# Two rows of maxima issued from ScalarE's queue, and two more banks in a ring of score banks

## The chip, the cores and the metric

The kernel runs on one core of a Trainium2 chip. The metric is the device time of one execution in microseconds. Engines are named as the profile names them: PE (TensorE, matmuls; PEld its weight loads), DVE (VectorE), ACT (ScalarE), POOL (GpSimd) and SP (SyncE, which here only issues DMAs). A queue is the list of instructions of one engine, taken in order.

## What is computed

Four layers on x of 2048 x 576: attention A, spectral layer B, and both again with the same weights. Only A is touched.

```python
def _A_ref(x, wqkv, wo):                      # on the layernorm of x
    B, S, D = x.shape
    H = 32; Dh = D // H; W = 256
    q, k, v = ...(x @ wqkv)...                 # 32 heads of 18
    scores = einsum("bhqd,bhkd->bhqk", q, k) * (Dh ** -0.5)
    mask = (idx[:, None] - idx[None, :] >= 0) & (idx[:, None] - idx[None, :] < W)
    p = softmax(where(mask, scores, -1e9))
    return einsum("bhqk,bhkd->bhqd", p, v)... @ wo
x = x + _A_ref(_layernorm(x), A_wqkv, A_wo)
x = x + _B_ref(_layernorm(x), ...)             # FFT, product, inverse FFT
```

## The kernel before

`layer_a` is called twice. Its first part normalises x, transposes it and makes v. Its second part, in which the change lies, is one loop over steps t (line 908), from -10 to 129. The 32 heads form 8 groups n of 4; a group has 16 tiles of 128 positions, and step t stands for tile j = t mod 16 of group n = t // 16.

In a step t from 0 to 127, `exps` makes for each of four heads the scores of key tile j against the query tiles j to j+2 by one matmul into a PSUM bank (E, L843), ACT's exponential of it into the tile `P` (L844), and POOL masks `P` (L846, L849). `pv` (L863) multiplies the `P` of two steps earlier with v into the bank `U`. In the same step `score_max` runs ten tiles ahead, for tile x = t + 10: a matmul of raw scores into a bank (S, L811) and a masked maximum over keys by DVE (L813) into a column of `m`. So the ten steps before step 0, called the lead here, hold maxima alone. After every fourth tile, `m_rows` transposes a chunk of 16 columns of `m` (four heads, four tiles; `tpm`, L819), ACT negates them into `mt` (L821), and four DMAs of 2 KB, one per head, put them as an extra row into the query tile `qs` (L826), where the matmul of E adds them to the scores, the keys holding ones in that row. E of step j needs the rows of query tile j+2: steps 0 and 1 need chunk 0, steps 2 to 5 chunk 1, steps 6 to 9 chunk 2. Chunks 0 and 1 of group 0 are finished in the lead, in steps -6 and -2. Every fourth step also has `norm`, which divides the results of a chunk (`tpo`, L873, L876, L878) and stores them to `o_d` (L883).

The projections to q and k (`proj`, L750) run in pieces between the steps up to step 102; `goal` says how many pieces stand after which step. Each ends in two banks `pj`, which ACT copies (L758), DVE adds (L762) and POOL splits into high and low part (`sg`, L763, L764); the result is stored to `qk_d` in DRAM (512 KB, L765) and comes back, sorted by head, as twelve loads of 72 KB per group and chunk (`stack_load`, L790, six for `qs`, six for `ks`). For the pieces made in the lead, `sg` lies in the five buffers of `P`: the exponentials of steps 0 to 4 each overwrite one of them and so wait until its store has landed. `sg2_0` is the projection piece i = 2, c = 0, and so on; `mt0_1` is group 0, chunk 1.

PSUM has 8 banks: three with the tag S, two E, two pj, one U. `bank` gives S, E, `tpm` and `tpo` their banks; in the lead S alone, from step 0 a ring of five: S, S, E, E, S.

Instructions stand on each engine in the order in which the code is written; nothing moves them but the code. Where a DMA is issued from, SP's queue or ACT's, is written in the code as well. The program that is built gives each such DMA one of eight completion counters, DMAHW0 to DMAHW7, in turn, one count for both queues, in an order of the whole program that the build chooses; a DMA waits until the DMA before it on its counter has landed.

At the end, `room` (step 104) loads the output projection's weights `wo` (L474, 2.9 MB a layer), and in steps 125 to 127 `turn` takes pj banks for transposes of the output (`tpa`, L499, L500, read by DVE in L504, L505).

Of the kernel before, what the change touches and what calls it, by code (L numbers as in the profile page):

```python
# [8 lines left out]
F32 = mybir.dt.float32  # L9
# [6 lines left out]
S, D = 2048, 576  # L16
# [559 lines left out]
def layer_a(tc, src, dst, wqk_d, wv_d, wo_d, dc_d, gc_d, dram, copy, wvs, wos, second, spectral):  # L576
    nc = tc.nc
# [8 lines left out]
    with ExitStack() as ctx:  # L586
# [129 lines left out]
        with ExitStack() as c2:  # L716
            wp = c2.enter_context(tc.tile_pool(name="a2", bufs=2))
            pp = c2.enter_context(tc.tile_pool(name="a2p", bufs=2, space=PSUM))
# [7 lines left out]
            for j in range(2):  # L726
                q = wp.tile([128, 2, S], F32R, name=f"qs{j}", bufs=1)
# [41 lines left out]
                            rest()  # L769
                return [lambda s=s, k=k: mm(s, k) for s, k in enumerate(ks)]  # L770

            turns, later = [0], []

            def bank(name):

                turns[0] += t >= 0
                return pp.tile([128, 512], F32, name=name, **(dict(tag="E", bufs=2) if turns[0] % 5 > 2 else dict(tag="S", bufs=3)))

            vts = {}

            def stack_load(n, c):

                q, k = qs[n % 2], ks_[n % 2]
                cs = slice(c * 512, c * 512 + 512)
                for which, t, parts in ((0, q, (0, 0, 1)), (1, k, (0, 1, 0))):
                    for hp in range(2):
                        r0 = 144 * n + 72 * which + 36 * hp
                        for slot, part in enumerate(parts):
                            b = 64 * hp + 18 * slot
                            nc.sync.dma_start(t[b:b + 18, :, cs].bitcast(F32),  # L790
                                              qk_d[part, r0:r0 + 36, cs].rearrange("(f d) t -> d f t", f=2).bitcast(F32))

            def v_load(n):
                v = wp.tile([128, NT, 4, 19], F32, tag="vq", name=f"vq{n}", bufs=2)
                nc.sync.dma_start(v.rearrange("p b h e -> p (b h e)"), v_d[n].rearrange("p b e -> p (b e)"))
                vts[n] = v
# [3 lines left out]
            def score_max(x, pair, hp):  # L800

                n, i = divmod(x, NT)
                c, t = divmod(i, 4)
                q, k = qs[n % 2], ks_[n % 2]
                if t == hp == pair == 0:
                    ms[n, c] = wp.tile([128, 2, 2, 4], F32, tag="m", name=f"m{n}_{c}", bufs=3)
                lo, hi = max(0, i - 2) * 128, (i + 1) * 128
                N = hi - lo
                b = 64 * hp
                ps = bank(f"S{x}_{pair}_{hp}")  # L810
                T.matmul(ps[:, 0:N], q[b:b + 63, pair, i * 128:i * 128 + 128], k[b:b + 63, pair, lo:hi], start=True, stop=True)  # L811
                jk = wp.tile([128, 384], BF, tag="jk", name=f"jk{x}_{pair}_{hp}", bufs=3)
                V.tensor_tensor_reduce(out=jk[:, 0:N], in0=ps[:, 0:N], in1=mask[:, 384 - N:384], scale=1.0, scalar=-3e38,  # L813
                                       op0=ALU.add, op1=ALU.max, accum_out=ms[n, c][:, hp, pair, t:t + 1])

            def m_rows(n, c):
                q = qs[n % 2]
                tp = bank(f"tpm{n}_{c}").rearrange("p (a t) -> p a t", a=4)
                T.transpose(tp[0:16, 0], ms[n, c].rearrange("p a b t -> p (a b t)"), ident)  # L819
                mt = wp.tile([16, 128], F32R, tag="mt", name=f"mt{n}_{c}", bufs=2)  # L820
                A.activation(mt, tp[0:16, 0], AF.Copy, scale=-1.0)  # L821
                for hp in range(2):
                    for pair in range(2):
                        r = (hp * 2 + pair) * 4
                        b = 64 * hp + 63
                        nc.sync.dma_start(q[b:b + 1, pair, c * 512:c * 512 + 512].rearrange("a (t q) -> a t q", t=4).bitcast(F32),  # L826
                                          mt[r:r + 4].bitcast(F32))

            pt = {}

            def exps(x, pair, hp):

                n, j = divmod(x, NT)
                q, k = qs[n % 2], ks_[n % 2]
                nq = min(3, NT - j) * 128
                hl_ = 2 * hp + pair
                if hp == pair == 0:
                    pt[n, j] = wp.tile([128, 4, 384], F32, tag="P", name=f"P{n}_{j}", bufs=5)
                p = pt[n, j]

                ps = bank(f"E{x}_{hl_}")
                b = 64 * hp
                T.matmul(ps[:, 0:nq], k[b:b + 64, pair, j * 128:j * 128 + 128], q[b:b + 64, pair, j * 128:j * 128 + nq], start=True, stop=True)  # L843
                A.activation(p[:, hl_, 0:nq], ps[:, 0:nq], AF.Exp, scale=SC)  # L844
                if hp == pair == 1:
                    P.affine_select(out=p[:, :, 0:128], in_=p[:, :, 0:128], pattern=[[0, 4], [1, 128]], compare_op=ALU.is_ge,  # L846
                                    fill=0.0, base=0, channel_multiplier=-1)
                    if nq == 384:
                        P.affine_select(out=p[:, :, 256:384], in_=p[:, :, 256:384], pattern=[[0, 4], [-1, 128]], compare_op=ALU.is_gt,  # L849
                                        fill=0.0, base=0, channel_multiplier=1)  # L850
# [45 lines left out]
            pj = [f for i in range(2, 9) for c in range(4) for f in proj(i, c, "E" if i == 2 and c % 2 else "pj", True)]  # L896
            done = 0

            goal = {t: -(-70 * (t + LEAD + 1) // 9) if t < -1 else (75, 80, 84)[t + 1] for t in range(-LEAD, 2)}
            for m in range(22):  # L900
                a, b = [2 + 23 * z // 5 for z in (m, m + 1)]
# [6 lines left out]
            for t in range(-LEAD, NX + 2):  # L908

                if t + LEAD in (0, 2):  # L910
                    stack_load(0, 2 + (t + LEAD) // 2)
                n, c = divmod(t + 20, NT)
                if c % 4 == 0 and 0 < n < NQ:
                    stack_load(n, c // 4)
                if t + LEAD == 5:
                    v_load(0)
                if t + 12 in range(NT, NX, NT):
                    v_load((t + 12) // NT)

                want = goal.get(t, len(pj))  # L920
                more, done = pj[done:want], want
                for pair in range(2):
                    for hp in range(2):
                        if 0 <= t < NX:
                            exps(t, pair, hp)
                    for hp in range(2):
                        if t + LEAD < NX:
                            score_max(t + LEAD, pair, hp)
                    while later:
                        later.pop()()  # L930
                    if pair == 0 and 0 <= t - 2 < NX:
                        pv(t - 2)
                    if pair == 0 and t < 2:
                        for f in more[:(len(more) + 1) // 2]:
                            f()
                        more = more[(len(more) + 1) // 2:]
                for f in more:
                    f()
                if copy and t >= 32 and t % 4 == 0 and t < 32 + 16 * len(copy):

                    z, r = divmod(t // 4 - 8, 4)
                    P.dma_start(*[a[32 * r:32 * r + 32] for a in copy[z]])

                y = t + LEAD - 1
                if 0 <= y < NX and y % 4 == 3:
                    m_rows(*divmod(y // 4, 4))
                y = t - 3
                if 0 <= y < NX - 1 and y % 4 == 3:
                    norm(*divmod(y // 4, 4))
                if t == OB - 16:  # L950
                    out.room()
                if t - OB in (0, 1, 2):
                    out.load(t - OB)
                if t == OB + 3:
                    out.consts()
                    out.last(slice(96, 128), slice(0, 56))
                if t == NX - 1:
                    out.last(slice(0, 96), slice(0, 128))

                if t - OB - 4 in (0, 1, 2, 4):  # L960
                    out.tail(min(t - OB - 4, 3))
                if t - OB - 5 in (0, 1, 2):
                    u = t - OB - 5
                    out.turn(u, pp.tile([128, 512], F32, tag="pj", name=f"tpa{u}", bufs=2), V)
                    if u < 2:
                        out.load(u + 3)
                if t == NX:

                    A.activation(wp.tile([128, 1], F32, name="se", bufs=1), eps, AF.Sqrt)
# [61 lines left out]
```

## Time and profile before

| | us |
|---|---|
| runs | 1547.83, 1542.71, 1542.78; median 1542.78 |
| the profiled execution | 1542.73 |
| its span, first to last instruction | 1540.7 |
| PE busy in the span | 1403.2 (91%) |
| DVE, ACT, POOL busy | 962.1, 815.6, 726.1 |
| matmuls E / S (L843 / L811), 1024 each | 233.2 / 234.2 |
| DVE masked maxima (L813), 1024 | 500.0 |
| ACT exponentials (L844), 1024 | 423.2 |

In the first attention layer, E of step 0 starts 132.32 us after the span's start, step 103 at 429.62, step 112 at 453.13 and step 118 at 468.15; in the second layer the same steps start at 901.38, 1198.03, 1221.55 and 1236.60.

How to read it: a row of a timeline gives start, length, engine, line, operation, out<-in, shape and count, and in brackets the idle time of the engine ahead of it with what ended it. A row of a windows table gives the stretch, its length, busy time and number of instructions of PE, PEld, DVE, ACT and POOL, then PE's granted clock as a share of full speed, the busy share of the DMA engines, and GB/s. A row of waits gives who waited for whom, the total, how many times, and the longest. Rows with a q behind the engine's name (SPq) are issues of DMAs: their length is the time of issue, not of the transfer.

### The profile page before, as it was taken

To read this page: it belongs to the slowest core of one execution; us is meant where nothing else is said; L and a number is where in the kernel's file an instruction comes from. 1 tells how busy PE (TensorE), PEld (TensorE's weight loads), DVE (VectorE), ACT (ScalarE), POOL (GpSimd) and SP (SyncE) were. 2 spreads that over 40 slices of the span, in tenths; PEclk is the share of its full clock that TensorE was granted. 3 is DMA by queue.
4 is the path that set the end of the run, shared out by engine and by line. 5 is a ranking of instruction groups with operands and counts; after the bars stand their busy time and mean duration, and the time that the engine had idled before them with its cause. 6 is when DMAs were issued, how large, how long until landed. Compare 5 with 4: busy or idle time off the path is not lost. (4 is left out here: it accounts for less than half of the span.)

```text
span 1540.7 us, 35484 instructions
## 1 busy us (share of the span) xinstructions
PE 1403.2 (91%) x12312; PEld 1071.6 (70%) x12312; DVE 962.1 (62%) x3103; ACT 815.6 (53%) x1895; POOL 726.1 (47%) x1215
## 2 busy tenths in 40 slices
PE   7997999999999899877789979999999998998677
PEld 7985666666656798537689856666666567985376
DVE  5356787788884555445443567878888835554445
ACT  6523767677666444225455236777666654442254
POOL 3364566566544333244611646565555443332445
PEclk9998999999999999988989989999999999999889
DMA  7856456555555366666374565555445553656663
GB/s 235 266 172 213 151 166 183 165 169 160 158 166 151 123 219 199 224 198 203 135 226 114 178 212 152 163 157 155 147 140 156 158 150 119 223 191 224 194 207 135
DMA packets 197423, 271.81 MB, mean 176 GB/s; under 512 B 87294, under 2 KB 109438, under 8 KB 196030
## 3 DMA queue, kind: packets, MB, share of 16 engines
q1 hardware_dynamic: 185502, 250.65, 52.3%
q10 hardware_dynamic: 10976, 15.59, 3.0%
q0 software_dynamic: 768, 3.31, 0.8%
q8 instruction: 99, 1.62, 0.5%
q14 instruction: 78, 0.64, 0.1%
HBM read 167.88 MB, written 103.86 MB: 176 GB/s over the span
## 5 line engine op out<-in xcount | busy, mean ns | idle before, releaser
L813 DVE CUSTOM_DVE_ANT_0 jk<-S,mask 128x384 bf16<-128x384 f32 (+2 forms) x1024 | 500.0, 529 | 111.5 <-PE S L811 106.9
L844 ACT ACTIVATE P<-E 128x384 f32<-128x384 f32 (+2 forms) x1024 | 423.2, 476 | 187.2 <-PE E L843 157.0
L846 POOL TENSOR_SCALAR_AFFINE_SELECT P<-P 128x512 f32<-128x512 f32 x256 | 162.3, 634 | 295.2 <-ACT P L844 277.8
L843 PE MATMUL E<-qs,ks 64*128 64x384 f32 (+2 forms) x1024 | 233.2, 400 | 21.8 <-DMA qs<-mt 15.3
L811 PE MATMUL S<-ks,qs 63*128 63x384 f32 (+2 forms) x1024 | 234.2, 367 | 3.3 <-DMA wqr<-in_wqk 1.9
L863 PE MATMUL U<-P,vq 128*19 128x128 f32 (+1 forms) x3840 | 202.9, 329 | 1.0 <-POOL P L849 1.0
L843 PEld LDWEIGHTS E<-qs,ks 64*128 64x128 f32 x1024 | 123.9, 184 | 106.2 <-issue 44.3
L750 PE MATMUL pj<-xh,wqh 64*128 64x512 f32 (+1 forms) x640 | 165.9, 405 | 2.1 <-ACT vt L710 1.7
L811 PEld LDWEIGHTS S<-ks,qs 63*128 63x128 f32 x1024 | 130.8, 186 | 44.8 <-ACT P L844 20.3
L863 PEld LDWEIGHTS U<-P,vq 128*19 128x19 f32 x3840 | 89.9, 98 | 93.5 <-issue 34.5
L849 POOL TENSOR_SCALAR_AFFINE_SELECT P<-P 128x512 f32<-128x512 f32 x224 | 142.0, 634 | 0.0
L750 PE MATMUL pj<-xl,wqh 64*128 64x512 f32 (+1 forms) x512 | 128.4, 395 | 0.0
L750 PE MATMUL pj<-xh,wql 64*128 64x512 f32 (+1 forms) x640 | 120.6, 392 | 0.0
L522 PE MATMUL ops<-oroom 128*128 128x288 f32 x784 | 113.7, 301 | 4.4 <-DVE oroom L505 3.0
L522 PEld LDWEIGHTS ops<-oroom 128*128 128x128 f32 x784 | 106.6, 191 | 6.2 <-DVE oroom L505 4.0
L171 POOL TENSOR_TENSOR eo<-xn 128x287 f32<-128x287 f32 x32 | 26.1, 817 | 148.2 <-ACT xn L169 148.2
L750 PEld LDWEIGHTS pj<-xh,wqh 64*128 64x128 f32 (+1 forms) x640 | 88.0, 188 | 7.4 <-ACT vt L710 2.1
L813 DVE DVE_READ_ACCUMULATOR2_ANT m<- 128x1 f32 x1024 | 85.0, 83 | 0.0
L199 PE MATMUL pf<-dc,et 128*128 128x290 f32 x384 | 72.4, 313 | 9.6 <-DVE et L190 6.5
L750 PEld LDWEIGHTS pj<-xh,wql 64*128 64x128 f32 (+1 forms) x640 | 72.2, 186 | 7.7
L764 POOL TENSOR_TENSOR sg<-sg 128x512 fp32r<-128x512 f32 x56 | 72.0, 1286 | 4.7
L750 PEld LDWEIGHTS pj<-xl,wqh 64*128 64x128 f32 (+1 forms) x512 | 71.3, 189 | 3.7
(181 smaller groups left out, 2555.4 us busy)
## 6 DMA issues: line engine op xcount, KB each, us to landing
qk_d<-sg SPq DMA_DIRECT2D x56, 512.0 KB
qs<-qk_d SPq DMA_DIRECT2D x384, 72.0 KB
ks<-qk_d SPq DMA_DIRECT2D x384, 72.0 KB
v_d<-vt SPq DMA_DIRECT2D x32, 304.0 KB
vq<-v_d SPq DMA_DIRECT2D x16, 608.0 KB
yd<-ye SPq DMA_DIRECT2D x32, 290.0 KB
wt<-in_w SPq DMA_DIRECT2D x16, 580.0 KB
x<-ofree SPq DMA_DIRECT2D x32, 288.0 KB
```

What stands on the lines that cost most here:

```text
L171: P.tensor_add(eo[:, 0, 1:288], xn[:, 1:288], xn[:, 575:288:-1])
L199: T.matmul(o, et[:, c, si], m(5 * c + mi), start=q == 0, stop=False)
L522: self.nc.tensor.matmul(self.ps[u][n][:, 0:288], x, self.w[p][:, wk * D + n * 288:wk * D + n * 288 + 288], start=first and i == 0, stop=la ...
L750: T.matmul(ps, w[r, wk], xT(xk, cs)[r], start=s == 0, stop=s == len(ks) - 1)
L764: (P if halves else V).tensor_sub(sg[:, 1], su, sg[:, 0].bitcast(F32))
L811: T.matmul(ps[:, 0:N], q[b:b + 63, pair, i * 128:i * 128 + 128], k[b:b + 63, pair, lo:hi], start=True, stop=True)
L813: V.tensor_tensor_reduce(out=jk[:, 0:N], in0=ps[:, 0:N], in1=mask[:, 384 - N:384], scale=1.0, scalar=-3e38, op0=ALU.add, op1=ALU.max, accu ...
L843: T.matmul(ps[:, 0:nq], k[b:b + 64, pair, j * 128:j * 128 + 128], q[b:b + 64, pair, j * 128:j * 128 + nq], start=True, stop=True)
L844: A.activation(p[:, hl_, 0:nq], ps[:, 0:nq], AF.Exp, scale=SC)
L846: P.affine_select(out=p[:, :, 0:128], in_=p[:, :, 0:128], pattern=[[0, 4], [1, 128]], compare_op=ALU.is_ge, fill=0.0, base=0, channel_mult ...
L849: P.affine_select(out=p[:, :, 256:384], in_=p[:, :, 256:384], pattern=[[0, 4], [-1, 128]], compare_op=ALU.is_gt, fill=0.0, base=0, channel ...
L863: T.matmul(U[32 * h:32 * h + 19, (q0 % 4) * 128:(q0 % 4) * 128 + 128 * (q1 - q0)], vts[n][:, j, h], pt[n, j][:, h, (q0 - j) * 128:(q1 - j) ...
```

## The change

Two edits. The rows of chunks that are finished before step 2, which are chunks 0 and 1 of group 0 in each layer, are issued from ACT's queue. And the ring becomes a list that is turned; after the last step with a projection (102), the two pj banks are put at its head, so that it has seven banks from step 103 on.

```diff
-            turns[0] += t >= 0
-            return pp.tile([128, 512], F32, name=name, **(dict(tag="E", bufs=2) if turns[0] % 5 > 2 else dict(tag="S", bufs=3)))
+            banks, later = ["S", "S", "E", "E", "S"], []
+            def bank(name):
+                tag = "S"
+                if t >= 0:
+                    banks.append(tag := banks.pop(0))
+                return pp.tile([128, 512], F32, name=name, tag=tag, bufs=3 if tag == "S" else 2)
...
-                        nc.sync.dma_start(q[b:b + 1, pair, c * 512:c * 512 + 512].rearrange("a (t q) -> a t q", t=4).bitcast(F32),
-                                          mt[r:r + 4].bitcast(F32))
+                        (nc.sync if t >= 2 else nc.scalar).dma_start(q[b:b + 1, pair, c * 512:c * 512 + 512].rearrange("a (t q) -> a t q", t=4).bitcast(F32),
+                                                                     mt[r:r + 4].bitcast(F32))
...
+                if t == max(goal) + 1:
+                    banks[:0] = ["pj", "pj"]
```

No instruction changes its place on PE, DVE or POOL. On ACT, in the first layer, eight DMAs come in (names in brackets are what an instruction waits for; lines are two higher than before):

```order
L823 ACTIVATE mt0_0_1483<-tpm0_0_1481 16x128 [waits PE_49]
L828 DMA qs0_1051<-mt0_0_1483 1x4x128 [waits DMAHW1_49,Activation_49,Pool_49]
L828 DMA qs0_1051<-mt0_0_1483 1x4x128 [waits DMAHW2_49]
L828 DMA qs0_1051<-mt0_0_1483 1x4x128 [waits DMAHW4_49]
L828 DMA qs0_1051<-mt0_0_1483 1x4x128 [waits DMAHW5_49]
L758 COPY sg2_2_1505<-pj2_2_0_1434 128x512 [waits PE_49]
L758 COPY sg2_3_1585<-pj2_3_0_1507 128x512 [waits PE_49]
L758 COPY sg3_0_1646<-pj3_0_0_1587 128x512 [waits PE_49]
L823 ACTIVATE mt0_1_1654<-tpm0_1_1652 16x128 [waits PE_49]
L828 DMA qs0_1051<-mt0_1_1654 1x4x128 [waits DMAHW1_49,Activation_49,Pool_49]
L828 DMA qs0_1051<-mt0_1_1654 1x4x128 [waits DMAHW3_49]
L828 DMA qs0_1051<-mt0_1_1654 1x4x128 [waits DMAHW4_49]
```

A twelfth row of the kind, the fourth DMA of `mt0_1`, waits for DMAHW6, and behind it stands the first exponential of step 0. Before, the same rows of ACT held the two `mt` and the three copies alone. On SP the loads of the last chunk of group 0 and the stores behind them now read:

```order
L792 DMA ks0_1052<-qk_d_70 18x2x512 [waits DMAHW7_49]
L792 DMA ks0_1052<-qk_d_70 18x2x512 [waits DMAHW0_49]
L792 DMA ks0_1052<-qk_d_70 18x2x512 [waits DMAHW1_49]
L792 DMA ks0_1052<-qk_d_70 18x2x512 [waits DMAHW2_49]
L792 DMA ks0_1052<-qk_d_70 18x2x512 [waits DMAHW3_49]
L792 DMA ks0_1052<-qk_d_70 18x2x512 [waits DMAHW4_49]
L765 DMA qk_d_70<-sg2_0_1348 128x2x512 [waits DMAHW5_49,Pool_49]
L765 DMA qk_d_70<-sg2_1_1420 128x2x512 [waits DMAHW6_49,Pool_49]
L604 DMA wqr5_1463<-in_wqk 128x640 [waits DMAHW7_49,Pool_49]
L797 DMA vq0_1489<-v_d_71 128x1216 [waits DMAHW0_49]
L765 DMA qk_d_70<-sg2_2_1505 128x2x512 [waits DMAHW1_49,Pool_49]
```

Before, four rows `qs0<-mt0_0` stood between `wqr5` and `vq0`, and the loads waited for other loads of SP. In the change, the DMAs ahead of the third, fifth and sixth load on their counters (1, 3, 4) are the first three DMAs of `mt0_1` on ACT, and the one ahead of the store of `sg2_1` (6) is the fourth; the counters' values in the built program say so. In the same way the last four loads of the chunk before wait, three of them, for DMAs of `mt0_0`.

On PE, the second place is step 113: the E and S matmuls of heads 0 and 2, those of U with the `P` of steps 110 and 111 between them, and E and S of heads 1 and 3. In the change it reads:

```order
L845 MATMUL E113_0_7791<-qs1_1053,ks1_1054 128x384 [waits Activation_49]
L845 MATMUL E113_2_7794<-qs1_1053,ks1_1054 128x384 [waits DVE_49]
L813 MATMUL S123_0_0_7797<-ks1_1054,qs1_1053 128x384 [waits DVE_49]
L813 MATMUL S123_0_1_7801<-ks1_1054,qs1_1053 128x384 [waits Activation_49]
L865 MATMUL U_1055<-P6_14_7655,vq6_6304 19x256 [waits Pool_49]
L865 MATMUL U_1055<-P6_14_7655,vq6_6304 19x256 x3
L865 MATMUL U_1055<-P6_15_7713,vq6_6304 19x128 [waits Pool_49]
L865 MATMUL U_1055<-P6_15_7713,vq6_6304 19x128 x3
L845 MATMUL E113_1_7815<-qs1_1053,ks1_1054 128x384 [waits Activation_49]
L845 MATMUL E113_3_7818<-qs1_1053,ks1_1054 128x384 [waits DVE_49]
L813 MATMUL S123_1_0_7823<-ks1_1054,qs1_1053 128x384 [waits DVE_49]
L813 MATMUL S123_1_1_7827<-ks1_1054,qs1_1053 128x384 [waits Activation_49]
```

The same matmuls before:

```order
L843 MATMUL E113_0_7791<-qs1_1053,ks1_1054 128x384 [waits DVE_49]
L843 MATMUL E113_2_7794<-qs1_1053,ks1_1054 128x384 [waits Activation_49]
L811 MATMUL S123_0_0_7797<-ks1_1054,qs1_1053 128x384 [waits Activation_49]
L811 MATMUL S123_0_1_7801<-ks1_1054,qs1_1053 128x384 [waits DVE_49]
L863 MATMUL U_1055<-P6_14_7655,vq6_6304 19x256 [waits Pool_49]
L863 MATMUL U_1055<-P6_14_7655,vq6_6304 19x256 x3
L863 MATMUL U_1055<-P6_15_7713,vq6_6304 19x128 [waits Pool_49]
L863 MATMUL U_1055<-P6_15_7713,vq6_6304 19x128 x3
L843 MATMUL E113_1_7815<-qs1_1053,ks1_1054 128x384 [waits DVE_49]
L843 MATMUL E113_3_7818<-qs1_1053,ks1_1054 128x384 [waits Activation_49]
L811 MATMUL S123_1_0_7823<-ks1_1054,qs1_1053 128x384 [waits Activation_49]
L811 MATMUL S123_1_1_7827<-ks1_1054,qs1_1053 128x384 [waits DVE_49]
```

The order is the same, and each matmul now waits for the reader of the bank seven back, an exponential or a maximum of the step before, where it waited for the one five back.

More of the change, by code (lines that the diff above doesn't have):

```diff
@@ L770, in proj @@
                 return [lambda s=s, k=k: mm(s, k) for s, k in enumerate(ks)]
-            turns, later = [0], []
+            banks, later = ["S", "S", "E", "E", "S"], []
             def bank(name):
-                turns[0] += t >= 0
-                return pp.tile([128, 512], F32, name=name, **(dict(tag="E", bufs=2) if turns[0] % 5 > 2 else dict(tag="S", bufs=3)))
+                tag = "S"
+                if t >= 0:
+                    banks.append(tag := banks.pop(0))
+                return pp.tile([128, 512], F32, name=name, tag=tag, bufs=3 if tag == "S" else 2)
             vts = {}
```

## Prediction

> **What bounds the kernel now.** I start from the page, whose first line is the profiled execution's span.
>
> ```profile
> span 1540.7 us, 35484 instructions
> ```
>
> That execution took 1542.73 us, so 2.0 us lie outside its span; it stands 0.05 us under the median of the three runs, 1542.78. The sum below is made against 1542.73. Next I read the list of waits for the tile that the change touches, the rows of maxima `mt`.
>
> ```profile
> PE E L843 <- DMA qs<-mt: 15.3, 2, 7.8
> ```
>
> Two waits, one in each attention layer, 15.3 us together. The timeline of PE shows the first of them, at step 2 of the first layer; the last row is step 6.
>
> ```profile
> 144.87 1.02 PE L843 MATMUL E<-qs,ks 64*128 64x384 f32 x2 [7.85 <-DMA qs<-mt]
> ...
> 145.82 1.02 PE L843 MATMUL E<-qs,ks 64*128 64x384 f32 x2
> ...
> 157.51 0.44 PE L843 MATMUL E<-qs,ks 64*128 64x384 f32 x2
> ```
>
> So PE stands from 137.0 to 144.9. The windows around it (the seventh column is the granted clock) show what the stall costs behind itself.
>
> ```profile
> 137.00:139.00 2.00, 0.02 (x2) 0.00 (x0) 1.32 (x5) 0.58 (x1) 1.79 (x3) 1.00 0.59 166
> 141.00:143.00 2.00, 0.00 (x0) 0.00 (x0) 0.00 (x0) 0.00 (x0) 0.00 (x0) 0.50 1.02 382
> 149.00:151.00 2.00, 2.00 (x22) 0.96 (x21) 0.65 (x3) 1.14 (x3) 0.00 (x0) 0.59 0.78 233
> ```
>
> The clock is half from 141 to about 150.5, so some 5.5 us of work run at half speed and lose about half of that. I put 1.9 us of it on the wait, as the steps after it are not all bound by the clock: 9.7 us a layer hang on these rows.
>
> Why are they late? SP's own timeline, in order of issue, and the two engines that feed it:
>
> ```profile
> 123.08 2.62 SPq L790 DMA_DIRECT2D ks<-qk_d  x6
> 125.80 0.89 SPq L765 DMA_DIRECT2D qk_d<-sg  x2
> ...
> 128.01 2.96 SPq L826 DMA_DIRECT2D qs<-mt  x4
> ...
> 131.99 3.13 SPq L790 DMA_DIRECT2D qs<-qk_d  x6
> 136.03 3.93 SPq L790 DMA_DIRECT2D ks<-qk_d  x6
> 140.06 0.90 SPq L765 DMA_DIRECT2D qk_d<-sg  x2
> 141.05 3.15 SPq L826 DMA_DIRECT2D qs<-mt  x4
> ...
> 149.71 2.50 SPq L826 DMA_DIRECT2D qs<-mt  x4
> ```
> ```profile
> 120.27 0.27 ACT L821 ACTIVATE mt<-tpm 16x128 fp32r<-16x128 f32 x1 [3.56 <-PE tpm L819]
> 121.34 0.59 ACT L758 COPY sg<-pj 128x512 f32<-128x512 f32 x1 [0.81 <-PE pj L750]
> ...
> 130.15 0.26 ACT L821 ACTIVATE mt<-tpm 16x128 fp32r<-16x128 f32 x1
> 132.81 0.87 ACT L844 ACTIVATE P<-E 128x384 f32<-128x384 f32 x2 [2.40 <-issue]
> ```
> ```profile
> 122.72 0.68 DVE L762 TENSOR_TENSOR sg<-sg,pj 128x512 f32<-128x512 f32 x1
> ```
>
> The rows of chunk 1 are ready on ACT at 130.41 and issued at 141.05: 10.6 us in SP's order, behind stores of projections and loads of the next group. That is the wait.
>
> **The lead, part by part.** *Removed from SP:* eight issues a layer, which took 2.96 + 3.15 = 6.1 us of its time. *Added to ACT:* the same eight, undisturbed 2.50 / 4 = 0.62 us each, so 2.5 us behind each `mt`. Chunk 0: ACT is free again at 123.0, and the copy of 121.34 is 1.7 us late; DVE's addition at 122.72 needs it, and starts about 1.0 us late, with the maxima queued behind it. I let between nothing and 0.7 us of this reach `mt` of chunk 1. Chunk 1: ACT issues until 132.9 or 133.6; the exponentials of 132.81 give way by under 1 us. Taken alone the rows of chunk 1 would land near 134.5, ahead of the 137.0 at which PE asks for them.
>
> *What takes the place of the wait.* SP and ACT draw the completion counters of their DMAs from the same eight, and a DMA waits until the one before it on its counter has landed. In the order of the change, the third, fifth and sixth of the six `ks` loads that stood at 123.08 follow the first three `mt` rows of chunk 1 on their counters, and the second store of `sg2` follows the fourth. So those loads, and all behind them on SP, now wait for rows that ACT issues after 130.4. The third row is issued at about 131.7 to 132.4 and ends 0.6 later. To land it takes at most 1.6 us: in the trace it was issued by 143.6 and the second matmul of the pair at 144.87, which needs it, had started before 145.82; I take 1.5. So it lands at 133.8 to 134.5, and the stores of 125.80 go out at about 134.2 to 134.9, over 8 us late.
>
> The rest of SP's chain, from those stores to the first row of chunk 2, took 149.71 - 125.80 = 23.9 us; without the eight issues, 17.8. So chunk 2 is issued from 152.0 to 152.7 instead of 149.71, and is usable 3.8 us later (as 141.05 to 144.87): step 6, which needs it, starts at 155.8 to 156.5 where it now starts at 157.51. PE itself would be there sooner: exponentials of step 0 overwrite the tiles that those stores read. Two stores and a row behind them were through in 4.8 us (140.06 to 144.87), so they hold step 0 until 137 to 139, PE stands about 4 us there once its banks are full, and 3.3 us for the rest of steps 0 and 1 (132.8 to 137.0, less the first pair) and 12.6 us for steps 2 to 5 (144.87 to 157.51) bring it to about 153.5. Chunk 2 is what comes last, and the layer gains 1.0 to 1.7 us of the 9.7; I take 1.2.
>
> Ends: the two groups of six loads at 131.99 and 136.03 took 7.1 us with their waits; if these shrink by 2.5 us, chunk 2 and PE's own path meet at 153.7, a gain of 3.8. If instead the stores and loads, now closer together, delay each other by 3 us more, the layer loses 2. So -3.8 to +2 a layer, nearer the first estimate since it keeps the chain's measured length; **-2.4 for both**.
>
> The Trainium skill, DMA: Bandwidth & Descriptors, section Issuing engines are not separate DMA queues, says that issuing from several engines saves only the sequencer's time of issue. By that rule the move would be worth at most the 6.1 us of SP's time a layer, -12.2 in all; by the rows above ACT's queue does pass 10.6 us of SP's order, and the counters take it back. No run here shows a row on ACT's queue.
>
> **The ring after step 102.** Steps 103 on, by windows (PE, PEld, DVE, ACT, POOL):
>
> ```profile
> 440.00:451.00 11.00, 10.24 (x104) 5.64 (x105) 9.30 (x37) 7.40 (x21) 4.92 (x9) 1.00 0.88 307
> ...
> 453.00:468.00 15.00, 13.91 (x135) 7.69 (x133) 12.98 (x52) 10.59 (x27) 6.74 (x11) 1.00 0.12 23
> 468.00:472.00 4.00, 3.69 (x47) 1.96 (x43) 1.82 (x8) 3.40 (x10) 1.80 (x3) 1.00 0.02 6
> 472.00:484.00 12.00, 10.67 (x141) 5.61 (x129) 0.71 (x2) 11.46 (x30) 8.38 (x16) 1.00 0.63 177
> ```
> ```profile
> 455.46 0.33 PE L843 MATMUL E<-qs,ks 64*128 64x384 f32 x1
> 456.02 0.44 PE L843 MATMUL E<-qs,ks 64*128 64x384 f32 x1 [0.23 <-ACT P L844]
> ```
>
> No engine is full, and the second E of a pair starts 0.56 us after the first: its bank waits for the exponential five banks back. Seven banks remove that. But up to step 112 the gain cannot be kept:
>
> ```profile
> 441.72 1.94 SPq L474 DMA_DIRECT2D oroom<-wos  x4
> 443.90 2.49 SPq L826 DMA_DIRECT2D qs<-mt  x4
> ```
> ```profile
> SPq L826 <- DMA oroom<-wos: 5.3, 4, 1.7
> ```
> ```profile
> 453.13 0.74 PE L843 MATMUL E<-qs,ks 64*128 64x384 f32 x2
> ```
>
> Step 112 (453.13) needs the rows issued at 443.90, which stand behind the loads of `wo` on one queue, and later rows wait for those loads. SP's order there starts from stores of step 102, before the longer ring, and PE is at step 112 just as the rows come. So steps 103 to 111 gain 0 to 0.6 a layer; this also covers step 103, whose second E now waits for DVE to leave the bank of the last projection (about 1 us).
>
> From 453 to 468 the floor is DVE, 12.98 of 15.0: at most 2.0 us to win, and I take three quarters, 1.5. From 472 on ACT is at 11.46 of 12 and nothing is to be had; 468 to 472 adds 0.3. Against that stands the end of the stage:
>
> ```profile
> 487.87 0.33 PE L843 MATMUL E<-qs,ks 64*128 64x128 f32 x2
> ```
> ```profile
> 487.88 0.56 DVE L505 TENSOR_TENSOR oroom<-tpa,oroom 128x384 fp32r<-128x384 f32 x1
> ```
>
> The last E of the last step now takes a bank that a transpose of the output holds until this DVE row ends at 488.44: about +0.5. So **-1.5 a layer (-2.8 to 0), -3.0 for both**.
>
> The Trainium skill, TensorE: Matmul & The Clock Gate, section A second HAM failure mode, tells of a kernel whose cycling through banks made the clock fall between bursts; by it the longer ring would win clock as well. Here the clock reads 1.00 in all four windows, and that term is zero.
>
> **The sum:** 1542.73 - 2.4 - 3.0 = 1537.3 us.
>
> **The rivals.**
> *The counters do not bind.* If the loads behind them are early enough not to matter, each layer keeps 9.7 and 9.3 us and the tail 3.0: 1520.7 us. For it: the rows are ready at 130.41. Against: the order places the waits as told. 0.11.
> *SP's chain shrinks.* The 3.8 us a layer and the tail's 2.8: 1529.5 us. For it: the six at 123.08 took 2.62 us, those at 131.99 and 136.03 took 3.13 and 3.93. 0.16.
> *The ring gains nothing*, since DVE or the last steps hold the tail: -2.4 alone, 1540.3 us. 0.12.
> *Slower: the late stores of SP hold the exponentials.* Steps 0, 1, 2 and 3 each wait for one of the four late stores; PE then stands twice for over 3.4 us (the clock fell between 139 and 143 after standing from 137.0) and steps 2 to 5 run at half clock throughout. Step 6 then starts at 161, +3.5 a layer, and with no gain in the tail the time is 1549.7 us. It decides if the third row of chunk 1 lands after about 138. 0.06.
>
> **How the numbers follow.** The forecast itself holds 0.55, from 1533 to 1543 with 0.08 of it under 1535. About 0.5% or 7.7 us is what a measurement of this kernel can tell from no change, so faster means under 1535.1 and slower over 1550.5. Faster: 0.11 + 0.16 + 0.08 = 0.35. Slower: 0.04, the upper part of the last rival. Same: 0.61. The range runs from 1528 to 1547: it takes in the bounds of both terms and leaves out 0.11 + 0.06.
>
> **What would show it.** Right: the wait for `qs<-mt` at step 2 is gone; SP's third `ks` load of the second six is issued after 132; PE stands near step 0 for `P`, and once more near step 3 or 6; step 6 of the first layer starts at 155 to 157; step 112 starts at the same distance from 443.90's rows as now, with a wait of 1 to 3 us; steps 112 to 118 take 13 to 14 us for 15.0. Wrong: step 6 before 153 or after 159, SP's stores before 130, or E without waits in steps 103 to 112 and earlier than now.

## The result, and the profile after

The changed kernel takes 1.0066 times the time of the kernel before (95% interval 1.0047 to 1.0085): slower by about 10 us, 1553.0 us (median of 7) against 1543.0 (7). The forecast was 1537.3. The profiled execution took 1552.06 us, and 9.3 us of its span are new:

```profile
span 1550.0 us, 35500 instructions
```

The list of waits has the two long waits of E for its rows gone, as intended (15.3 us before). In their place ScalarE's exponentials wait for the stores of projections, and SP's loads wait for the rows:

```profile
ACT P L846 <- DMA qk_d<-sg: 21.2, 5, 7.4
...
PE E L845 <- DMA qs<-mt: 7.1, 4, 2.7
```
```profile
SPq L792 <- DMA qs<-mt: 13.7, 6, 4.1
```

Neither the first nor the third of these rows stands in the profile of before. The third is the cause and the first the cost; the experiments below test that. SP's timeline in the first layer shows where the hold sits (start and length of issue):

```profile
119.63 5.11 SPq L792 DMA_DIRECT2D ks<-qk_d  x6
124.79 3.44 SPq L792 DMA_DIRECT2D qs<-qk_d  x6
128.45 6.65 SPq L792 DMA_DIRECT2D ks<-qk_d  x6
135.20 1.09 SPq L765 DMA_DIRECT2D qk_d<-sg  x2
...
138.40 0.43 SPq L765 DMA_DIRECT2D qk_d<-sg  x1
...
156.77 2.62 SPq L828 DMA_DIRECT2D qs<-mt  x4
...
165.75 2.89 SPq L828 DMA_DIRECT2D qs<-mt  x4
```

The six `ks` loads that took 2.62 us before take 6.65, and the six of the chunk before, at 119.63, take 5.11 (3.09 before): each group waits for rows of a chunk that ScalarE issues only then. The first two stores go out at 135.20 instead of 125.80. A second effect comes with it. The rows take counters out of SP's turn, so that an SP load can stand behind another SP load that was issued only four loads earlier: the load of 119.31 waits until that of 114.79 has landed, at 119.29. Up to the first store SP waits 7.2 us for rows and 4.2 us for its own loads of `qs` and `ks`, where the latter was 1.7 before. ScalarE's timeline has both ends of it, the rows (ACTq) and the exponentials that write over the stored tiles:

```profile
119.65 3.13 ACTq L828 DMA_DIRECT2D qs<-mt  x4
122.83 0.58 ACT L758 COPY sg<-pj 128x512 f32<-128x512 f32 x1 [3.25 <-DMA qs<-mt]
...
131.51 2.46 ACTq L828 DMA_DIRECT2D qs<-mt  x4
138.52 1.76 ACT L846 ACTIVATE P<-E 128x384 f32<-128x384 f32 x4 [7.39 <-DMA qk_d<-sg]
...
145.77 1.64 ACT L846 ACTIVATE P<-E 128x384 f32<-128x384 f32 x4 [1.40 <-POOL sg L763]
...
152.16 1.64 ACT L846 ACTIVATE P<-E 128x384 f32<-128x384 f32 x4 [2.49 <-DMA qk_d<-sg]
```

These are the exponentials of steps 0, 2 and 3, each held by another store. (The middle one is put down to POOL, which had long finished `sg2_2`; that tile's store landed at 145.66 by the trace, 0.1 us ahead of it.) PE stands behind each of them, and once more at step 10, whose rows are the four issued at 165.75:

```profile
139.06 0.69 PE L845 MATMUL E<-qs,ks 64*128 64x384 f32 x1 [4.34 <-ACT P L846]
...
146.31 0.44 PE L845 MATMUL E<-qs,ks 64*128 64x384 f32 x1 [1.62 <-ACT P L846]
...
152.71 0.43 PE L845 MATMUL E<-qs,ks 64*128 64x384 f32 x1 [1.25 <-ACT P L846]
...
160.57 0.44 PE L845 MATMUL E<-qs,ks 64*128 64x384 f32 x2
...
173.44 0.82 PE L845 MATMUL E<-qs,ks 64*128 64x384 f32 x2 [1.74 <-DMA qs<-mt]
```

Step 6 starts at 160.57, where before it started at 157.51. The windows of the changed kernel, with clock and DMA share in the seventh and eighth columns, say why three short waits cost so much:

```profile
130.00:134.00 4.00, 3.72 (x27) 2.37 (x25) 3.52 (x14) 0.74 (x2) 2.78 (x3) 1.00 0.09 28
134.00:138.00 4.00, 0.72 (x8) 0.35 (x4) 0.96 (x4) 0.00 (x0) 0.00 (x0) 0.82 0.68 238
138.00:142.00 4.00, 2.94 (x15) 2.56 (x17) 1.38 (x5) 2.35 (x6) 1.22 (x2) 0.50 1.01 254
142.00:146.00 4.00, 2.69 (x17) 1.91 (x13) 3.35 (x13) 1.95 (x5) 1.98 (x4) 0.83 0.79 297
146.00:150.00 4.00, 3.69 (x16) 2.23 (x16) 1.09 (x6) 1.68 (x5) 2.35 (x3) 0.60 0.62 207
150.00:154.00 4.00, 2.75 (x26) 1.55 (x26) 1.48 (x5) 1.64 (x4) 0.13 (x1) 0.93 0.74 237
154.00:158.00 4.00, 4.00 (x36) 2.43 (x34) 2.20 (x11) 1.60 (x4) 1.09 (x2) 0.62 0.69 216
```

The same windows of before:

```profile
130.00:134.00 4.00, 3.78 (x28) 3.06 (x29) 3.53 (x14) 1.29 (x4) 2.08 (x3) 1.00 0.75 204
...
138.00:142.00 4.00, 0.00 (x0) 0.00 (x0) 0.36 (x1) 0.00 (x0) 2.13 (x3) 0.80 0.63 204
```

The clock falls three times instead of once, and recovers in between. And the DMA engines, 0.75 busy in 130 to 134 before, stand at 0.09 while SP is held, and are full (1.01) in 138 to 142, when the stores are wanted.

In the tail, step 112 now waits for its rows, and the last matmul of the last step for a transpose; the windows stand around the first of them:

```profile
461.51 1.04 PE L845 MATMUL E<-qs,ks 64*128 64x384 f32 x2 [2.73 <-DMA qs<-mt]
...
497.26 0.29 PE L845 MATMUL E<-qs,ks 64*128 64x128 f32 x1 [0.40 <-DVE oroom L505]
```
```profile
458.00:461.50 3.50, 0.78 (x16) 0.34 (x7) 2.03 (x9) 0.45 (x2) 0.64 (x1) 0.90 0.75 248
461.50:465.50 4.00, 3.99 (x28) 2.44 (x28) 1.29 (x5) 1.44 (x4) 0.00 (x0) 0.50 0.19 35
```

PE was ready for step 112 2.73 us sooner, and then ran it and step 113 at a clock of 0.50.

This table gives, for every profile here, how many us longer (or, with a minus, shorter) than before each stretch of steps took, first layer / second layer, by the starts of the steps' first matmuls on PE's timeline. "-10" is the first S of a layer. From step 32 to 102 no profile differs by more than 1.0 us. The kernels are described with the experiments.

| kernel | -10 to 2 | 2 to 6 | 6 to 32 | 102 to 112 | 112 to 118 | 118 to 127 |
|---|---|---|---|---|---|---|
| the change | -0.9 / -0.7 | 4.3 / 4.9 | 5.1 / 0.7 | 0.3 / -0.5 | 0.1 / -0.9 | 0.2 / 0.2 |
| rows_alone | 1.6 / -0.1 | 4.7 / 5.3 | 5.5 / 0.6 | 0.9 / 0.0 | -0.2 / 0.0 | 0.0 / 0.0 |
| rows_c1 | 1.5 / 2.3 | 2.8 / 0.5 | 6.1 / 2.0 | 0.0 / 0.0 | 0.0 / 0.0 | 0.0 / 0.0 |
| rows_c0 | 3.6 / 3.4 | 0.2 / 0.8 | 0.1 / 0.0 | 0.0 / 0.3 | 0.0 / -0.2 | 0.0 / 0.0 |
| rows_pool | -7.3 / -6.8 | -0.1 / 1.3 | 1.9 / 1.5 | 1.3 / 0.4 | -0.2 / -0.2 | 0.0 / 0.0 |
| sp_order | -5.5 / -3.7 | 0.8 / 2.2 | 2.5 / 2.8 | 0.0 / 0.1 | 0.0 / -0.1 | 0.0 / 0.0 |
| rows_freed | -6.7 / -6.4 | 5.6 / 4.8 | 1.7 / 3.0 | 0.0 / 0.0 | 0.0 / 0.0 | 0.0 / 0.0 |
| order_freed | -8.9 / -7.6 | 6.3 / 7.5 | 1.9 / 3.7 | 0.7 / 0.3 | -0.2 / -0.2 | 0.0 / 0.0 |
| ring_alone | 0.2 / 1.0 | 0.5 / 0.4 | 1.5 / 0.0 | 0.8 / -0.8 | 0.4 / -0.9 | 0.2 / 0.2 |
| ring_room114 | -0.6 / 0.0 | -0.6 / -0.6 | 0.5 / 0.1 | -2.6 / -2.6 | -2.1 / -2.1 | 3.9 / 2.9 |
| ring_row106 | 0.8 / 2.1 | -0.3 / 0.1 | 1.8 / 0.0 | -2.6 / -2.6 | -2.1 / -2.1 | -0.7 / -0.7 |
| pool_ring | -6.5 / -2.6 | 1.7 / 0.3 | 1.4 / 1.5 | -2.6 / -2.6 | -2.1 / -2.0 | -0.7 / -0.7 |
| pool2_ring | -6.3 / -3.9 | 0.8 / -0.8 | 2.0 / 1.9 | -2.6 / -2.6 | 0.7 / -1.5 | -0.7 / -0.7 |

It has its own scatter: where the lead wasn't touched (the three kernels whose names begin with ring), the first three columns add up to between -0.7 and 2.3 a layer. What lies between the layers and behind the second varies as well, by several us from profile to profile. In the change the columns add up to 8.5 and 4.9 us for the two leads and to 0.6 and -1.2 for the tails; the span is 9.3 us longer.

### The profile page after: what moved, and what is told of

It is laid out like the page before. It is cut to its first block, busy times and chain, and to the rows that moved or that the text cites. A ratio compares the mean times of both kernels' runs of the same rounds, so it can differ in the third digit from the quotient of the medians.

```text
span 1550.0 us, 35500 instructions
## 1 busy us (share of the span) xinstructions
PE 1405.0 (91%) x12312; PEld 1073.0 (69%) x12312; DVE 959.5 (62%) x3103; ACT 815.5 (53%) x1895; POOL 725.9 (47%) x1215
## 3 DMA queue, kind: packets, MB, share of 16 engines
q8 instruction: 99, 1.62, 0.5%
## 5 line engine op out<-in xcount | busy, mean ns | idle before, releaser
L845 PE MATMUL E<-qs,ks 64*128 64x384 f32 (+2 forms) x1024 | 229.2, 401 | 25.3 <-ACT P L846 15.0
L813 PE MATMUL S<-ks,qs 63*128 63x384 f32 (+2 forms) x1024 | 238.5, 370 | 7.0 <-DVE m L815 3.2
L865 PE MATMUL U<-P,vq 128*19 128x128 f32 (+1 forms) x3840 | 207.2, 335 | 2.1 <-POOL P L851 2.0
L813 PEld LDWEIGHTS S<-ks,qs 63*128 63x128 f32 x1024 | 133.8, 190 | 49.8 <-ACT P L846 23.0
```

The costliest lines, as they stand in the source:

```text
L865: T.matmul(U[32 * h:32 * h + 19, (q0 % 4) * 128:(q0 % 4) * 128 + 128 * (q1 - q0)], vts[n][:, j, h], pt[n, j][:, h, (q0 - j) * 128:(q1 - j) ...
```

## The experiments

The theory: ScalarE's rows hold SP through the completion counters, SP's stores come late, and the exponentials wait for them. The rivals: ScalarE's time for issuing is the cost; the longer ring is the cost; or nothing but SP's order matters, whichever queue the rows take. Each ratio is against runs of the kernel before on the same chip.

**The parts alone.** `rows_alone` leaves the join of the pj banks out, `ring_alone` the other queue:

```diff
-                if t == max(goal) + 1:
-                    banks[:0] = ["pj", "pj"]
```
```diff
-                        (nc.sync if t >= 2 else nc.scalar).dma_start(
+                        nc.sync.dma_start(
```

> The rows of chunks 0 and 1 from ScalarE's queue, without the longer ring. If the counters cost the time (SP's loads and stores wait for the rows on ScalarE): the lead as in the changed kernel, step 13 later than before by 6 to 7 us in the first layer and by about 4 in the second, ScalarE's exponentials waiting some 20 us in all for the stores of sg, and a time of 1551 to 1556 us. If the ring costs it: 1543 us or less, and no such waits.

Measured: 1.0047 (1.0021 to 1.0073), by the ratio 1550.0 us, just under the range given. Step 13, counted from step -10, is 11.6 and 5.7 us later, more than expected. The waits are those of the change:

```profile
ACT P L846 <- DMA qk_d<-sg: 24.5, 6, 7.7
```
```profile
SPq L792 <- DMA qs<-mt: 15.0, 6, 5.3
```

> The longer ring from step 103, with the rows on SP as before. If the lead carries the whole loss: 1540 us, between 1538.5 and 1543, steps 103 to 111 faster by 2 to 3 us of which step 112 gives all back by waiting for its rows. If the ring is a part of the loss (the wait at step 112 lowers the clock, the last steps wait for transposes): 1545 to 1548 us.

Measured: 0.9997 (0.9975 to 1.0018). So the rows carry the loss, and the ring by itself shows neither a gain nor a loss. From step 103 to step 111 2.6 us are gained, and step 112 gives most or all of them back: in the first layer it waits 3.16 us for its rows. By the ratio the time is 1542.3 us, at the upper end of the range given for the theory; the interval, 1538.9 to 1545.5, reaches into the other range too, so this run alone does not decide between them.

**One chunk alone.** The condition becomes `t == -2` (chunk 1) or `t == -6` (chunk 0):

```diff
-(nc.sync if t >= 2 else nc.scalar)
+(nc.scalar if t == -2 else nc.sync)
```

> Only the rows of chunk 1 from ScalarE's queue, no longer ring. In the built program the third, fifth and sixth load ahead of SP's late stores still wait by their counters for these rows. If that hold is the whole loss: stores at 133 to 137 us, exponentials waiting some 20 us in all for them, step 13 later by 5 to 10 us in the first layer, 1550 to 1556 us. If the issuing of chunk 0 on ScalarE, ten steps earlier, is a large part: 1547 us or less.

Measured: 1.0087 (1.0064 to 1.0109), the slowest of all, by the ratio 1556.2 us, at the upper end of the range given. The hold is there, but another wait ends last than the one expected: exponentials wait 3.9 us for stores in all, not some 20. The rows of chunk 0, back on SP, stand behind the held stores, and step 0 waits for them:

```profile
135.19 0.89 SPq L765 DMA_DIRECT2D qk_d<-sg  x2
136.18 0.83 SPq L604 DMA_DIRECT2D wqr<-in_wqk  x1
137.10 2.63 SPq L828 DMA_DIRECT2D qs<-mt  x4
```
```profile
141.05 1.02 PE L845 MATMUL E<-qs,ks 64*128 64x384 f32 x2 [8.24 <-DMA qs<-mt]
```

> Only the rows of chunk 0 from ScalarE's queue, no longer ring; by the counters the loads now wait for rows that are issued from 120 us on. If the hold for chunk 1 is the loss: stores at 126 to 129 us, step 2 within 2 us of before, where it waits for its rows on SP as before, no exponential waits for a store, 1541 to 1548 us. If ScalarE's issuing by itself costs: 1550 us or more.

Measured: 1.0038 (1.0019 to 1.0057), so this too loses, against my expectation for the theory. Its waits and SP's stores show how:

```profile
SPq L792 <- DMA qs<-mt: 6.9, 3, 3.6
```
```profile
130.30 0.89 SPq L765 DMA_DIRECT2D qk_d<-sg  x2
```
```profile
148.39 1.01 PE L845 MATMUL E<-qs,ks 64*128 64x384 f32 x2 [9.25 <-DMA qs<-mt]
```

Chunk 0's rows make SP late as well, its first store by 4.5 us (130.30 for 125.80): up to it SP waits 3.6 us for those rows, and 4.3 instead of 1.7 for its own loads. Chunk 1's rows, on SP, come later with it: step 2 at 148.39 for 144.87. One exponential still waits 3.0 us for a store. I had taken the hold of chunk 1 for the whole of it. Each of the two chunks holds SP once.

**Other counters.** `rows_pool` issues the same rows from GpSimd's queue:

```diff
-(nc.sync if t >= 2 else nc.scalar)
+(nc.sync if t >= 2 else nc.gpsimd)
```

> The same rows from GpSimd's queue, whose DMAs have completion counters of their own; no longer ring. If the shared counters cost the time: SP's first two late stores go out at 122 to 127 us instead of 135, exponentials no longer wait for them, step 2 starts by 141 and the time is 1526 to 1538 us. If instead the rows on another queue cost it by themselves (the issuing engine held up, transfers crowding each other): the stores may be early, but the time stays at 1548 us or more.

Measured: 0.9948 (0.9927 to 0.9969), 1540.7 us beside 1547.6 for the kernel before on that chip (by the ratio 1534.7 against the profile's 1542.73, inside the range). In the trace GpSimd's DMAs count on eight semaphores of their own, where those of SP and ScalarE share eight others. The waits of the change are absent from its list, the stores are early, and PE waits briefly for chunk 1 and for chunk 2:

```profile
126.28 1.07 SPq L765 DMA_DIRECT2D qk_d<-sg  x2
```
```profile
138.35 0.41 PE L845 MATMUL E<-qs,ks 64*128 64x384 f32 x1 [1.14 <-DMA qs<-mt]
139.27 0.41 PE L845 MATMUL E<-qs,ks 64*128 64x384 f32 x1 [0.50 <-DMA qs<-mt]
150.93 0.76 PE L845 MATMUL E<-qs,ks 64*128 64x384 f32 x2 [0.86 <-DMA qs<-mt]
```

So a queue of its own does what the change was meant to do, where no counter ties it to SP. As the issuing leaves ScalarE too, this run by itself does not tell the counters from ScalarE's time.

**SP's order.** `sp_order` is the kernel before with `stack_load(1, 0)` moved behind the rows of chunk 1. `rows_freed` has the rows on ScalarE and moves that and `stack_load(0, 3)` there, so that the loads which chunk 1's rows hold by the counters no longer stand ahead of those stores; `order_freed` is that order with the rows on SP.

```diff
-                if t + LEAD in (0, 2):
-                    stack_load(0, 2 + (t + LEAD) // 2)
+                if t == -LEAD:
+                    stack_load(0, 2)
...
                     m_rows(*divmod(y // 4, 4))
+                if t == -2:
+                    stack_load(0, 3)
+                    stack_load(1, 0)
```

> The kernel before with one thing moved: on SP the first twelve loads of group 1 stand behind the rows of chunk 1 instead of ahead of them; rows stay on SP. If the place in SP's order is what made the rows late, they go out at 132 to 135 us, land before 140, and step 2 starts by 140 instead of 144.9; with chunk 2 now the next to come, 1530 to 1538 us. If SP's chain only moves its delay to chunk 2, steps 6 starts as before and the time is 1541 to 1545 us.

Measured: 0.9984 (0.9962 to 1.0006). By the ratio this is 1540.3 us, between the two ranges. Step 2 starts at 140.12, as expected, but of the 5.5 and 3.7 us won by then 2.2 are left at step 32 of the first layer and nothing at that of the second: rows of later chunks are late in turn.

```profile
140.12 0.93 PE L843 MATMUL E<-qs,ks 64*128 64x384 f32 x2 [2.14 <-DMA qs<-mt]
153.58 0.76 PE L843 MATMUL E<-qs,ks 64*128 64x384 f32 x2 [1.01 <-DMA qs<-mt]
```

> The rows of chunks 0 and 1 from ScalarE's queue, no longer ring, and the 24 loads of the last chunk of group 0 and the first of group 1 issued behind the stores of sg instead of ahead of them, so that what waits for the rows of chunk 1 by the counters are loads that nobody needs yet. If the counters' hold on SP's stores costs the time: no exponential waits for a store of sg for more than 1 us, step 2 starts by 141 and the time is 1530 to 1540 us. If ScalarE's issuing itself or the transfers' crowding costs it: exponentials and copies still late, 1547 us or more.

Measured: 0.9988 (0.9968 to 1.0008). With the rows on ScalarE the first store goes out at 126.12, no exponential waits for a store any more, and step 2 starts 5.5 us sooner than before. SP still waits 7.9 us for rows, but only 2.7 of it in the first layer ahead of the first store, for chunk 0. This speaks for the hold and against ScalarE's issuing as the main cost. But the time, 1540.9 us by the ratio, is just above the range: the moved loads are now late themselves, and S of step 2 waits for them.

```profile
144.23 0.66 PE L813 MATMUL S<-ks,qs 63*128 63x384 f32 x1 [4.49 <-DMA ks<-qk_d]
```

> The same order of SP, with the rows of both chunks on SP, where they now stand ahead of those 24 loads. If SP's order alone makes the rows late in the kernel before, this is as fast as the same order with ScalarE's queue, within 3 us: 1530 to 1542 us. If another queue is needed to pass the stores and loads, step 2 starts 3 us or more later than in that run.

Measured: 1.0011 (0.9986 to 1.0035), by the ratio 1544.4 us and outside its range. Its first store goes out at 120.82, 5.3 us ahead of `rows_freed`: with the rows on ScalarE, those of chunk 0 still made SP late there. Step 2 starts at 136.9, sooner than with ScalarE's queue; then S waits for the same loads, 4.98 us. The intervals of the two ratios overlap. With this order of SP the rows need no other queue to be in time, and being in time is not enough.

**The tail.** `ring_room114` is `ring_alone` with the loads of `wo` ten steps later. `ring_row106` has instead the rows of step 112 on GpSimd's queue, and takes the pj banks out of the ring at step 123:

```diff
-                if t == OB - 16:
+                if t == OB - 6:
                     out.room()
```
```diff
-(nc.sync if t >= 2 else nc.scalar)
+(nc.gpsimd if t == max(goal) + 4 else nc.sync)
...
+                if t == OB + 3:
+                    banks[:] = [k for k in banks if k != "pj"]
```

> The longer ring with the rows on SP, and the loads of the output's weights moved from step 104 to step 114, behind two more chunks of rows. If the rows stuck behind those loads take the ring's gain of steps 103 to 111: no wait of 2.7 us at step 112, PE's clock stays at full there, and steps 103 to 118 take 3 to 5 us less than before in each layer, 1534 to 1541 us. If the exponentials or the maxima bound these steps anyway: no more than 1 us a layer, 1541 to 1545 us; if the weights now come too late for the output: slower than 1545 us.

Measured: 0.9991 (0.9974 to 1.0008). Steps 102 to 118 take 4.7 us less in both layers, as expected; then 3.9 and 2.9 us are lost again up to step 127. Two things stand there. Step 122 waits for its rows, which are behind the weights, 1.67 us in the first layer and 1.21 in the second:

```profile
461.38 2.04 SPq L474 DMA_DIRECT2D oroom<-wos  x4
466.49 2.44 SPq L828 DMA_DIRECT2D qs<-mt  x4
```
```profile
471.89 0.79 PE L845 MATMUL E<-qs,ks 64*128 64x384 f32 x2 [1.67 <-DMA qs<-mt]
```

And from step 125 to step 127, among the transposes of the output, 1.9 and 2.8 us more pass than before; in 484 to 488 of the first layer the granted clock is 0.57. What makes them late was not isolated.

> The tail alone: the lead as before, the longer ring from step 103 to step 122, and only the rows of step 112 from GpSimd's queue, past the loads of the output's weights. If those rows and the last steps' transposes take the ring's gain: steps 103 to 127 take 4.5 to 5.5 us less than before in each layer, 1531 to 1537 us. If most of the gain of the kernel with both came from the lead: 1539 us or more.

Measured: 0.9942 (0.9923 to 0.9961), 1533.8 us by the ratio. Steps 102 to 127 take 5.3 us less in the first layer and 5.4 in the second; of this 0.7 lies behind step 118, where `ring_alone`, which keeps the banks in the ring, loses 0.2. The clock stays at 1.00 in the windows around step 112 (453.8), and from there on DVE is busy for 13.58 of 15.0 us:

```profile
444.00:454.00 10.00, 9.55 (x119) 5.67 (x111) 9.38 (x38) 7.10 (x22) 6.70 (x12) 1.00 0.92 315
454.00:469.00 15.00, 14.67 (x160) 8.61 (x158) 13.58 (x56) 12.37 (x33) 7.85 (x13) 1.00 0.24 55
```

**Both.** `pool_ring` is `ring_row106` with the rows of chunks 0 to 3 on GpSimd's queue as well (`t <= 6`), `pool2_ring` with those of chunks 0 and 1 (`t < 2`).

> Rows of chunks 0 to 3 of group 0 and of chunk 0 of the last group from GpSimd's queue, the longer ring from step 103 until step 122, after which the projections' banks leave it again. The lead as with chunks 0 and 1 on GpSimd's queue or up to 3 us a layer better, as chunk 2 no longer waits in SP's order; the tail better by 3 to 5 us a layer, as the rows of step 112 pass the loads of the output's weights and no matmul of the last two steps waits for a transpose: 1522 to 1533 us. If GpSimd's time for issuing holds up the masks of P: 1536 us or more.

Measured: 0.9865 (0.9826 to 0.9905), 1523.8 us beside 1547.1 for the kernel before on that chip: the fastest here, ahead of both kernels.

> As the kernel with rows of chunks 0 to 3 on GpSimd's queue and the ring until step 122, but with the rows of chunks 2 and 3 on SP again. If chunks 2 and 3 gained nothing there: within 2 us of it, 1522 to 1531 us. If the wait of step 6 for chunk 2 cost 3 us a layer: 1529 to 1535 us.

Measured: 0.9888 (0.9865 to 0.9910), 1528.1 us beside 1545.8. The intervals overlap, so chunks 2 and 3 on GpSimd's queue may be worth up to a few us, or nothing. PE's wait for rows in the two:

```profile
PE E L845 <- DMA qs<-mt: 2.8, 4, 1.5
```
```profile
PE E L845 <- DMA qs<-mt: 5.6, 9, 2.2
```

## Why the prediction was wrong

**The wait that goes, and the hold that comes: right, within 0.4 us.** The third row of chunk 1 was to be issued at 131.7 to 132.4 and to land at 133.8 to 134.5; by the trace it was issued at 132.78 and landed at 134.40. The stores were to go out at 134.2 to 134.9 and went at 135.20. PE was to stand about 4 us at step 0 and stood 4.34.

**Behind the stores: here the working failed.** "Two stores and a row behind them were through in 4.8 us ... so they hold step 0 until 137 to 139" was near the truth for the first two stores (landed at 138.41 and 140.57 by the trace), and I priced no wait for the other two. "3.3 us for the rest of steps 0 and 1" took 4.5 (139.06 to 143.59), with the clock at 0.50 up to 142. `sg2_2` was issued at 138.40 behind the weights `wqr` and the 0.6 MB of `vq`, and landed at 145.66; `sg2_3` landed at 152.06. So "12.6 us for steps 2 to 5" stood on a PE that waits once. It waited three times, the clock was at half or a little above in 138 to 142, 146 to 150 and 154 to 158, and steps 2 to 5 took 17.0 us (143.59 to 160.57). In the same way "the rest of SP's chain ... without the eight issues, 17.8" was a length measured while the DMA engines had been at work all along. Measured were 156.77 - 135.20 = 21.6 us. SP's loads wait 6.0 us in that stretch for earlier transfers on their counters, where they waited 2.8 before: I read this as what could not be transferred during the hold (DMA share 0.09 for 0.75), on top of what was due, but no run tests it alone. The rows of chunk 2 landed at 160.06 to 160.58, and PE came to step 6 at 160.57 with no wait for them. So both paths, forecast for 155.8 to 156.5 and for 153.5, ended there, and either of the two errors alone would have put step 6 there; "after 159" was among the forecast's own signs of being wrong. The term of -1.2 a layer had an end of +2, "if instead the stores and loads, now closer together, delay each other by 3 us more". Up to step 6 that end is about what happened: +2.4 us from step 0 to step 6 in the first layer and +3.4 in the second.

**Behind step 6: not priced at all.** The chain is still late when chunk 3 is due: its rows are issued at 165.75, and step 10 waits 1.74 for them in the first layer and drops the clock again, +3.6 by step 16 (+0.6 in the second). I had ended the working at chunk 2.

**Chunk 0: its price was in the wrong place.** I let at most 0.7 us of ScalarE's late copy reach `mt` of chunk 1. The copy was late as told (122.83 for 121.34), but more of it came through. From `mt` of chunk 0 to `mt` of chunk 1 pass 9.89 and 9.86 us before (first and second layer); with chunk 0's rows on ScalarE 11.56 and 11.01 in the change, 11.54 and 11.06 in `rows_c0`, 11.53 and 11.04 in `rows_freed`, 13.04 and 11.23 in `rows_alone`; with those rows on SP 9.85 to 9.89 in every run, and on GpSimd 9.86 to 10.43. So ScalarE's own issuing makes the rows of chunk 1 later by 1.1 to 1.7 us a layer, and once by 3.2. That its rows hold SP in just the way of chunk 1's stood in the order, but not in the sum; nor did SP's longer waits for its own loads. Alone chunk 0 costs 0.38%. In the change itself the stores go out when chunk 1's rows have landed, so that this delay is hidden behind theirs.

**The tail: the floor was right, its price was not.** Steps 102 to 112 were to gain 0 to 0.6 us and gave -0.3 and +0.5; the wait at step 112 was to be 1 to 3 us and is 2.73; from step 118 on 0.3 was to be gained, and steps 118 to 127 cost 0.2; at the very end 0.5 was to be lost, and the last matmul waits 0.40. But the 1.5 us from step 112 to step 118 came only in part (-0.1 and 0.9), as the wait dropped the clock to 0.50 for the next 4 us. In the lead I had counted such a drop behind a wait; here, where the wait was my own forecast, I had not. Without the wait the full 2.1 us come (`ring_row106`).

**The rivals.** "The late stores of SP hold the exponentials" is what happened, with its place and nearly its price (step 6 at 161, 1549.7 us; measured 160.57, and 1552.9 us by the ratio). Its condition was wrong, a third row that lands after about 138: it landed at 134.40, and the rival came all the same, since it hangs on the third and fourth store and not on the rows. Nor did PE have to stand for over 3.4 us: waits of 4.34, 1.62 and 1.25 us went with the three falls of the clock. So its chance, 0.06, was read off the wrong event. That the counters don't bind is refuted by the 13.7 us of SP's waits; `rows_pool`, where they don't, gained 8.0 us of the 19.0 that this rival gave the rows. By the table 14.1 us of it are won up to step 2, and 9.5 are left at step 32; part of the rest is the wait for chunk 2 (0.86 us at step 6 of the first layer).

The Trainium skill's rule in DMA: Bandwidth & Descriptors, section Issuing engines are not separate DMA queues, gave at most -12.2 us for the rows. The gain from GpSimd's queue, 8.0 us by the ratio, lies within it. In the tail the measurement goes beyond the rule: from step 102 to 118 `ring_row106` takes 5.7 and 3.0 us less than `ring_alone`, and issuing the four rows from SP took 2.49. There the place in SP's order was worth more than the time of issue.

**What stays open.** How much of the loss in time is ScalarE's own issuing, by way of that delay of 1.1 to 1.7 us, was not measured by itself: the one experiment with ScalarE's queue and no exponential held by a store brought a new wait. `rows_c1` shows that it isn't needed for a loss: there the delay is absent (9.86 in both layers), and it is the slowest. `rows_c0`'s 0.38% holds both prices of chunk 0 together. Why the span gives back 2.1 us behind the last step of the second layer in the change was not followed either.

## What to carry to other kernels

Before a DMA is moved to another queue, look in the built program at which DMAs come next on its completion counter: here a late DMA on ScalarE's queue held an early one on SP's, and all behind that. When a delay is pushed down a chain, price every consumer of the chain until it has caught up, with the transfers that pile up meanwhile, and count the fallen clock behind each wait that is forecast. Here a longer ring paid only when the next thing late (four rows of 2 KB behind 2.9 MB of weights) was moved in the same edit.

## What the runs showed of the hardware

Four rows cost GpSimd about as much to issue as the other engines (2.03 us in `ring_row106`, against 2.46 on ScalarE and 2.50 on SP), and on its queue they did not have to land behind the 2.9 MB of weights. Issued from 444.36 on, beside the weights on SP, they landed by 452.51, and the last of the weights at 456.67, by the trace; no matmul waited for them. In the change the rows, behind the weights on SP's queue, landed from 461.37 on, about when the last of the weights did (461.55). I had taken that landing for a floor of step 112.

```profile
444.36 2.03 POOL L828 DMA_DIRECT2D qs<-mt  x4
444.65 2.59 SPq L474 DMA_DIRECT2D oroom<-wos  x4
```

A single wait of PE of 2.73 us was enough for a granted clock of 0.50 in the 4 us behind it; in the lead, in the windows behind waits of 1.62 and 1.25 us, it read 0.60 and 0.62.
